# A long convolution with a gated projection on one core: PSUM tiles of one and two banks, one engine per first-stage group, GpSimd copying the real half

## The chip, the core and the metric

The kernel runs on one core of a Trainium2 chip. Five engines of the core work from queues of their own, each in order: TensorE (PE in the profile, with its weight loads as PEld) multiplies matrices, VectorE (DVE), ScalarE (ACT) and GpSimd (POOL) work elementwise, and SyncE (SP) issues the transfers between the large memory (HBM) and the on-chip memory SBUF. Matmuls write into a separate memory, PSUM, from which VectorE and ScalarE copy the results out; here it is cut into eight banks of 512 float32 values per partition. Engines wait for one another through semaphores, which the framework sets from the tiles that each instruction reads and writes.

The metric is the device time of one execution in microseconds, lower is better.

## The reference

Eight sequences of 6400 steps with 128 channels are convolved with a filter as long as they are, by a Fourier transform over twice the length; the result is gated and projected.

```python
def _attn_ref(x, h):                    # x (8, 6400, 128), h (6400, 128)
    L = 2 * S
    Xf = np.fft.rfft(x, n=L, axis=1)
    Hf = np.fft.rfft(h, n=L, axis=0)
    return np.fft.irfft(Xf * Hf[None], n=L, axis=1)[:, :S, :]

def _moe_ref(x, w_val, conv_w, w_out):  # x is the result above
    gate_pre[:, t] = sum over k of conv_w[k] * x[:, t - 4 + k]   # 5 taps, per channel
    gate = 1.0 / (1.0 + np.exp(-gate_pre))
    return (gate * (x @ w_val)) @ w_out
```

All arrays are float32.

## The kernel before

The length is split as 6400 = 100 x 64 (`N1`, `N2`), so that the transform becomes matmuls with small constant matrices, in four stages.

- **First stage** (`first_stage`, line 475): a transform of length 100 over one axis, in 16 groups of 8 channels per sequence. A group is 4 matmuls (8 instruction records in the trace, `ps<-r_sb,x`) into a *two-bank* PSUM tile; then four copies of 64 x 400 values bring it to `gy`, two by each of two steps `ev` (`j` = 0 and 1, one for each half of the partitions). Either step may go to ScalarE or VectorE.
- **Second stage** (`second`): a transform of length 64 for 13 groups `kb` of up to 8 frequencies, also into two banks (`ps<-gy,m`), followed by the product with the filter's spectrum. In `product` ScalarE copies the two halves, swapped, to a `w` tile, VectorE multiplies by the two spectrum tiles `h` (from HBM, 512 KB each), and GpSimd adds the two products into `gy`.
- **Third stage** (line 684 on): 32 groups of 4 channels, each 4 matmuls (8 records, `ps<-r_sb,gy`) into *one* bank, and one copy of 100 x 512 values to `dt` by ScalarE or VectorE.
- **Fourth stage**: 13 chunks of 5 (the first of 4) of the 64 columns (`ps<-m_sb,dt`), each into *one* bank; from that bank ScalarE and VectorE apply the five taps of the gate's convolution, with one addition by GpSimd. The function `gated` then applies the sigmoid, multiplies by the value projection (`ps<-y,w_sb`, *one* bank) and projects the product (`ps<-dt,w_sb` or `ps<-gl,w_sb`, *one* bank). Chunks from number 9 (`LAGGED`) on are copied out at once and finished later.

The **head** runs the first stage on the filter and on sequence 0, then 13 times `spectrum` (the filter's second stage, its real and imaginary halves written twice, once negated, to the `h` tiles and to HBM) with `direct` (sequence 0's second stage and product). In `spectrum` (line 611) ScalarE copies the real half from PSUM twice (`r0`, `r1_`) and the imaginary half negated (`i0`); GpSimd negates that in SBUF (`i1`). The first six groups of sequence 1 are stashed in the space of the table `m4`, and GpSimd copies them to `gy` later ("unstash").

After the head, for each sequence `b`: the third stage of `b` runs beside the first stage of `b + 1`, since the first stage overwrites parts of `gy` that the third stage has read, and then the fourth stage of `b` beside the second stage of `b + 1`. The third stage's copies to `dt` wait for all of the previous sequence's fourth stage and for its projections from `dt`.

**What sets the order.** Every step is added to a `_Plan` with a cost per engine it may run on, the steps it follows, a due time and its PSUM bank. `_Plan.forward` (line 196) simulates the engines with these costs: whenever an engine is free it takes the ready step that is due first and that fits. The order that comes out is written to the program, each instruction pinned behind those before it on its engine (`_InOrder`), so the chip keeps that order whatever its own times are. Due times come from the constants at the top: `PERIOD` per sequence, `THIRD`, `SECOND`, `FOURTH` for the spacing inside it, `GATE`, `LAGS`, `EARLY` for gating and chunks. The costs are `_act`, `_dve`, `_pool`, `_pe`, `_dma`.

**PSUM in the plan.** Four two-bank tiles (`places`, line 372) hold everything. `room` (line 309) gives a two-bank step the first pair of which both halves are free, and a one-bank step a half, a pair that is already half used first. A half is `places[i][:, h]`, a slice of the two-bank tile. `fits` keeps two engines from using a bank at the same time, except where their `side` masks differ, as those of the two first-stage `ev` steps do: the plan lets these run together.

Of the kernel before, what the change touches and what calls it, by code (L numbers as in the profile page):

```python
# [44 lines left out]
THIRD = 57000  # L45
FOURTH = 5150
SECOND = 4000
GATE = 15000
LAGS = 8200
EARLY = -1800  # L50
# [72 lines left out]
class _Op:  # L123
# [3 lines left out]
    def __init__(self, run, cost, after, bank=None, new=False, side=3, port=False):  # L127
        self.run, self.cost, self.bank, self.new, self.side, self.port = run, cost, bank, new, side, port
        self.after = [a for a in after if a is not None]
        self.rank = self.at = self.done = self.engine = None  # L130


class _Plan:
# [62 lines left out]
    def forward(self, places):  # L196
# [3 lines left out]
        halves = [[0] * 2 for _ in range(places)]  # L200
# [11 lines left out]
        def fits(o, e):  # L212
# [9 lines left out]
            return not any(x != e and s & o.side and t > now for x, s, t in b.seen)  # L222
# [5 lines left out]
        while left:  # L228
            moved = True
            while moved:  # L230
                moved = False
                for e in free:
# [27 lines left out]
                    if b is not None:  # L260
                        if o.new:
                            i, h = b.spot = self.room(b, halves, now)
                            for k in (0, 1) if b.n == 2 else (h,):
                                halves[i][k] = None
                        b.seen.append((e, o.side, now + dur))
# [10 lines left out]
                    heapq.heappush(events, (now + dur, -1, None))  # L276
                    moved = True
# [20 lines left out]
    def order(self, places):  # L298
        self.link()
        self.due()  # L300
        began, self.span = self.forward(len(places))
        for o in self.ops:
            if o.bank is not None:
                i, h = o.bank.spot
                o.bank.place = places[i] if o.bank.n == 2 else places[i][:, h]
        return began

    @staticmethod
    def room(b, halves, now):
        ok = [[t is not None and t <= now for t in p] for p in halves]  # L310
        if b.n == 2:
            return next(((i, 0) for i, p in enumerate(ok) if all(p)), None)
        one = [(i, p.index(True)) for i, p in enumerate(ok) if any(p)]
        return min(one, key=lambda x: (all(ok[x[0]]), x[0]), default=None)


def _act(n, ptr=False, held=False, sb=False):
    d = 150 + n / 1.2 + 95 * ptr + 45 * sb
# [26 lines left out]
def longconv_moe(ctx: ExitStack, tc: tile.TileContext, x, h, r1, m2, r3, m4, w64, out):  # L345
# [26 lines left out]
    places = [pp.tile([128, 2, 512], F32, name=f"ps_{i}") for i in range(4)]  # L372
# [102 lines left out]
    def first_stage(src, dst, before, base, step, groups=range(NG)):  # L475
        done = []
        for g in groups:
# [18 lines left out]
            for j in range(2):  # L496

                def ev(e, g=g, j=j, bank=bank):
                    v = bank.ap().rearrange("p b (m x) -> p b x m", x=SW)
# [459 lines left out]
```

## Time and profile before

| | us |
|---|---|
| median of 3 runs | 1389.91 (1385.95 to 1393.13) |
| the profiled execution | 1374.47 |
| its span, first to last instruction | 1372.7 |
| mean granted TensorE clock | 0.951 |
| one sequence, from one start of the fourth stage to the next (814.07 to 971.13) | 157.1 |

The profile comes from one execution; its time lies below the three runs of the table. The tables by stage give, for each stretch, the length, then for PE, PEld, DVE, ACT and POOL the busy time with the number of instructions, then the granted clock, the DMA share and the GB/s. A timeline row gives start, length, engine, line, operation, output and inputs, the number of merged instructions and, in brackets, how long the engine had been idle and what released it. Line 101 is the helper through which every instruction is issued, so groups are told apart by their tiles: `ps` is PSUM, buffer numbers are left out. PE is busy through most of the span; its busy time is that of pipelined matmuls, whose shown end includes some time that the next one overlaps.

### The profile page before, as it was taken

The page shows a single profiled execution, that of the slowest core. Times are in us where ns is not written, and L with a number is a line of the kernel's source. Part 1 is how long each engine was busy: PE and PEld are TensorE (multiplying, and loading weights), DVE is VectorE, ACT ScalarE, POOL GpSimd, SP SyncE. Part 2 cuts the span into 40 slices and gives each one's busy share as a digit, 9 for nine tenths or more (in the row PEclk, how much of TensorE's full clock was granted, in tenths as well). Part 3 has the DMA queues.
Part 4 walks back from the last instruction along what each step waited for, and adds up shares of the span by engine and source line. Part 5 has one row for each costly group of instructions (what it writes and reads, how often), then busy time and mean ns, then how long its engine had stood idle before and what let it go on. Part 6 is the DMA issues. An engine that isn't in the chain of part 4 may idle for free. (4 is left out here: it accounts for less than half of the span.)

```text
span 1372.7 us, 19881 instructions
## 1 busy us (share of the span) xinstructions
PE 1154.0 (84%) x7480; PEld 979.3 (71%) x7480; DVE 757.2 (55%) x1069; ACT 774.8 (56%) x1269; POOL 419.0 (31%) x239
## 2 busy tenths in 40 slices
PE   8986788788988889888887888888897888877785
PEld 8976787568875787668875787657875788755652
DVE  6874157643785358542775447652685437741254
ACT  5764467555764557455764557555673557633342
POOL 0396016410561016310462006510363105610011
PEclk9999999999999999699998999999997999989887
DMA  9578447722884248621684228732585217600011
GB/s 260 166 250 290 146 145 276 246 77 66 272 268 132 76 150 295 203 84 61 226 293 142 83 81 299 261 97 68 185 297 180 78 40 271 219 30 29 0 40 56
DMA packets 80460, 221.15 MB, mean 161 GB/s; under 512 B 9514, under 2 KB 24846, under 8 KB 80142
## 3 DMA queue, kind: packets, MB, share of 16 engines
q1 hardware_dynamic: 80366, 219.89, 49.3%
q8 instruction: 59, 0.97, 0.3%
q14 instruction: 35, 0.29, 0.1%
HBM read 184.47 MB, written 39.32 MB: 163 GB/s over the span
## 5 line engine op out<-in xcount | busy, mean ns | idle before, releaser
L101 PEld LDWEIGHTS ps<-r_sb,gy 128*100 128x100 f32 x2048 | 244.8, 173 | 100.9 <-ACT dt L101 37.9
L101 PEld LDWEIGHTS ps<-m_sb,dt 100*128 100x128 f32 x2048 | 258.7, 205 | 78.3 <-ACT w L101 16.8
L101 PE MATMUL ps<-r_sb,gy 128*100 128x128 f32 x2048 | 263.0, 278 | 51.4 <-ACT dt L101 22.5
L101 PE MATMUL ps<-m_sb,dt 100*128 100x100 f32 x2048 | 266.2, 290 | 42.1 <-ACT w L101 14.2
L101 DVE COPY gy<-ps 64x400 f32<-64x400 f32 x242 | 139.4, 576 | 287.9 <-ACT gy L101 284.2
L101 POOL TENSOR_TENSOR gy<-gy,w 128x1024 f32<-128x1024 f32 x96 | 239.0, 2495 | 143.8 <-DVE w L101 113.8
L101 ACT COPY dt<-ps 100x512 f32<-100x512 f32 (+2 forms) x286 | 160.7, 588 | 185.6 <-PE ps L101 164.0
L101 PE MATMUL ps<-r_sb,x 100*128 100x200 f32 x992 | 196.4, 344 | 46.6 <-issue 35.5
L101 PEld LDWEIGHTS ps<-gy,m 128*128 128x128 f32 x1600 | 195.2, 190 | 33.3 <-issue 16.0
L101 PEld LDWEIGHTS ps<-r_sb,x 100*128 100x128 f32 x992 | 169.7, 194 | 66.3 <-issue 55.9
L101 PE MATMUL ps<-gy,m 128*128 128x128 f32 x1600 | 204.1, 281 | 12.8 <-DVE gy L101 5.6
L101 DVE SCALAR_TENSOR_TENSOR dt<-ps,w_sb,dt 128x500 f32<-128x500 f32 (+7 forms) x216 | 133.3, 628 | 79.1 <-PE ps L101 51.1
L101 ACT COPY gy<-ps 64x400 f32<-64x400 f32 x246 | 119.3, 485 | 98.4 <-PE ps L101 93.8
L101 ACT COPY y<-ps 128x500 f32<-128x500 f32 x150 | 85.7, 576 | 120.0 <-PE ps L101 105.9
L101 ACT ACTIVATE w<-ps 64x1024 f32<-64x1024 f32 (+1 forms) x91 | 90.0, 989 | 84.1 <-DVE gy L101 47.8
L101 POOL TENSOR_TENSOR gl<-gl,q 128x500 f32<-128x500 f32 (+1 forms) x48 | 56.7, 1181 | 242.7 <-DVE gl L101 242.7
L101 DVE TENSOR_TENSOR gy<-ps,h 128x1024 f32<-128x1024 f32 (+1 forms) x100 | 116.3, 1173 | 18.9 <-PE ps L101 9.4
L101 DVE TENSOR_TENSOR w<-w,h 128x1024 f32<-128x1024 f32 (+1 forms) x91 | 126.4, 1399 | 0.0
L101 PE MATMUL ps<-y,w_sb 128*128 128x500 f32 x178 | 102.7, 661 | 17.5 <-DVE y L101 5.0
L101 POOL MEMSET dt<- 128x4 f32 x8 | 0.8, 105 | 378.0 <-PE ps L101 378.0
L101 POOL TENSOR_TENSOR dt<-dt,q 128x500 f32<-128x500 f32 (+1 forms) x64 | 84.5, 1320 | 101.2 <-DVE dt L101 101.0
L101 ACT COPY w<-ps 64x1024 f32<-64x1024 f32 (+2 forms) x95 | 90.7, 955 | 9.1 <-DVE dt L101 5.8
(53 smaller groups left out, 890.7 us busy)
## 6 DMA issues: line engine op xcount, KB each, us to landing
h<-hd SPq DMA_DIRECT2D x168, 512.0 KB, 4.8
m<-m SPq DMA_DIRECT2D x96, 512.0 KB, 5.2
x<-xl SPq DMA_DIRECT2D x116, 224.0 KB, 2.6
out<-y SPq DMA_DIRECT2D x89, 250.0 KB, 2.6
hd<-h SPq DMA_DIRECT2D x8, 512.0 KB, 3.5
hd<-hd SPq DMA_DIRECT2D x14, 256.0 KB, 3.8
h<-hd SPq DMA_DIRECT2D x14, 256.0 KB, 3.8
m_sb<-xl SPq DMA_DIRECT2D x12, 224.0 KB, 6.1
```

What stands on the lines that cost most here:

```text
L101: return self._tc.keep_in_program_order(call(*args, **kwargs))
```

## The change

- PSUM: two pair tiles stay. The other two pairs are tiles of a pool of their own in the head; at the first one-bank step this pool is closed and four one-bank tiles `pb_` take its place. `room` gives two-bank steps any pair before that moment and pairs 0 and 1 after it, and one-bank steps the four single tiles.
- First stage: one `ev` step makes all four copies of a group, on ScalarE or VectorE. The `side` masks are gone.
- `fits` counts a bank as in use until 45 ns (`HOP`) after an instruction on another engine ends.
- Head: GpSimd copies the real half in SBUF (after `r0`) in place of ScalarE's second PSUM copy, and ScalarE copies the imaginary half from PSUM in place of GpSimd's negation.
- Costs and constants: `_act`, the unstash cost, and six due-time constants. `PERIOD`, `HEAD_END` and all tile sizes in SBUF stay.

```diff
--- before.py
+++ after.py
@@ -42,12 +42,12 @@
 YB = 6
 HEAD_END = 101000
 PERIOD = 126600
-THIRD = 57000
-FOURTH = 5150
-SECOND = 4000
-GATE = 15000
-LAGS = 8200
-EARLY = -1800
+THIRD = 52500
+FOURTH = 5450
+SECOND = 4150
+GATE = 11750
+LAGS = 10260
+EARLY = -4600
 
 
 def _out_range(ch):
@@ -124,8 +124,8 @@
 
 
 
-    def __init__(self, run, cost, after, bank=None, new=False, side=3, port=False):
-        self.run, self.cost, self.bank, self.new, self.side, self.port = run, cost, bank, new, side, port
+    def __init__(self, run, cost, after, bank=None, new=False, port=False):
+        self.run, self.cost, self.bank, self.new, self.port = run, cost, bank, new, port
         self.after = [a for a in after if a is not None]
         self.rank = self.at = self.done = self.engine = None
 
@@ -193,11 +193,12 @@
                 if not need[id(u)]:
                     todo.append(u)
 
-    def forward(self, places):
+    def forward(self):
         need = {id(o): len(o.after) for o in self.ops}
         free = dict.fromkeys(("tensor", "scalar", "vector", "gpsimd", "sync"), 0)
         ready = {e: [] for e in free}
-        halves = [[0] * 2 for _ in range(places)]
+        halves = [[0] * 2 for _ in range(4)]
+        self.split = False
         port = server = now = 0
         events, began = [], []
         for o in self.ops:
@@ -219,7 +220,7 @@
                 return True
             if o.new:
                 return all(x.spot is not None for x in b.before) and self.room(b, halves, now) is not None
-            return not any(x != e and s & o.side and t > now for x, s, t in b.seen)
+            return not any(x != e and t > now for x, t in b.seen)
 
         for o in self.ops:
             if not need[id(o)]:
@@ -260,9 +261,10 @@
                     if b is not None:
                         if o.new:
                             i, h = b.spot = self.room(b, halves, now)
+                            self.split = self.split or b.n == 1
                             for k in (0, 1) if b.n == 2 else (h,):
                                 halves[i][k] = None
-                        b.seen.append((e, o.side, now + dur))
+                        b.seen.append((e, now + dur + self.HOP))
                         b.left -= 1
                         if not b.left:
                             i, h = b.spot
@@ -274,6 +276,7 @@
                     heapq.heappush(events, (o.done, self.index[id(o)], o))
                     heapq.heappush(events, (free[e], -1, None))
                     heapq.heappush(events, (now + dur, -1, None))
+                    heapq.heappush(events, (now + dur + self.HOP, -1, None))
                     moved = True
             if not left:
                 break
@@ -295,27 +298,25 @@
                 if not need[id(u)]:
                     wake(u)
 
-    def order(self, places):
+    def order(self):
         self.link()
         self.due()
-        began, self.span = self.forward(len(places))
-        for o in self.ops:
-            if o.bank is not None:
-                i, h = o.bank.spot
-                o.bank.place = places[i] if o.bank.n == 2 else places[i][:, h]
+        began, self.span = self.forward()
         return began
 
-    @staticmethod
-    def room(b, halves, now):
-        ok = [[t is not None and t <= now for t in p] for p in halves]
+    def room(self, b, halves, now):
+
+
+        free = [[t is not None and t <= now for t in p] for p in halves]
         if b.n == 2:
-            return next(((i, 0) for i, p in enumerate(ok) if all(p)), None)
-        one = [(i, p.index(True)) for i, p in enumerate(ok) if any(p)]
-        return min(one, key=lambda x: (all(ok[x[0]]), x[0]), default=None)
+            return next(((i, 0) for i, p in enumerate(free) if all(p) and (i < 2 or not self.split)), None)
+        if not self.split and not all(all(p) for p in free[2:]):
+            return None
+        return next(((i, h) for i in (2, 3) for h in (0, 1) if free[i][h]), None)
 
 
 def _act(n, ptr=False, held=False, sb=False):
-    d = 150 + n / 1.2 + 95 * ptr + 45 * sb
+    d = 155 + n / 1.2 + 112 * ptr + 35 * sb
     return d + 12 if held else d - 85, d
 
 
@@ -369,7 +370,10 @@
     x_sb = [cp.tile([PX, XG, N2], F32, name=f"x_{i}") for i in range(XB)]
     w_t = [cp.tile([128, KB * C], F32, name=f"w_{i}") for i in range(WB)]
     q_t = [cp.tile([128, CH, N1], F32, name=f"q_{i}") for i in range(2)]
-    places = [pp.tile([128, 2, 512], F32, name=f"ps_{i}") for i in range(4)]
+    early = tc.tile_pool(name="ep", bufs=1, space=bass.MemoryType.PSUM)
+    places = [[p.tile([128, 2, 512], F32, name=f"ps_{i}")] for p, i in ((pp, 0), (pp, 1))]
+    ep = early.__enter__()
+    places += [[ep.tile([128, 2, 512], F32, name=f"ps_{i}")] for i in (2, 3)]
     hd = dp.tile([NKB, 2, 2 * N2, KB * C], F32, name="hd")
     hx = h_sb + [dt[:, N1 * C + i * KB * C : N1 * C + (i + 1) * KB * C] for i in range(2)]
 
@@ -493,18 +497,18 @@
 
             p = add(mm, {"tensor": _pe(338, 4)}, [loads[n], r1_in], bank=bank, new=True)
             firsts.append(p)
-            for j in range(2):
-
-                def ev(e, g=g, j=j, bank=bank):
-                    v = bank.ap().rearrange("p b (m x) -> p b x m", x=SW)
+
+            def ev(e, g=g, bank=bank):
+                v = bank.ap().rearrange("p b (m x) -> p b x m", x=SW)
+                for j in range(2):
                     for c in range(2):
                         copiers[e](
                             dst(g)[c * N2 : (c + 1) * N2, 2 * j : 2 * j + 2],
                             v[j * N2 : (j + 1) * N2, :, c * N1 : (c + 1) * N1],
                         )
 
-                cost = {"scalar": _times(_act(400, held=True), 2), "vector": _times(_dve(400, held=True), 2)}
-                done.append(add(ev, cost, [p, *before(g)], bank=bank, side=1 << j))
+            cost = {"scalar": _times(_act(400, held=True), 4), "vector": _times(_dve(400, held=True), 4)}
+            done.append(add(ev, cost, [p, *before(g)], bank=bank))
         return done
 
 
@@ -617,12 +621,12 @@
         old = [hx_user[2 * kb + r - len(hx)] if kb >= 3 else [] for r in range(2)]
         cost = {"scalar": _act(n, held=True)}
         r0 = add(lambda e: nc.scalar.copy(t[0][:N2], v()[:N2]), cost, [p, *old[0]], bank=bank)
-        r1_ = add(lambda e: nc.scalar.copy(t[0][N2:], v()[:N2]), cost, [p, *old[0]], bank=bank)
+        r1_ = add(
+            lambda e: nc.gpsimd.tensor_copy(hs[0][N2:, :n], hs[0][:N2, :n]),
+            {"gpsimd": (170 + 0.86 * n,) * 2}, [r0, *old[0]],
+        )
         i0 = add(lambda e: nc.scalar.activation(t[1][:N2], v()[N2:], AF.Copy, scale=-1.0), cost, [p, *old[1]], bank=bank)
-        i1 = add(
-            lambda e: nc.gpsimd.tensor_scalar(out=hs[1][N2:, :n], in0=hs[1][:N2, :n], scalar1=-1.0, scalar2=None, op0=MUL),
-            {"gpsimd": (1250, 1250)}, [i0, *old[1]],
-        )
+        i1 = add(lambda e: nc.scalar.copy(t[1][N2:], v()[N2:]), cost, [p, *old[1]], bank=bank)
         full = kb < WHOLE
         st = [dma(hd[kb, 0, : 2 * N2 if full else N2, :n], hs[0][: 2 * N2 if full else N2, :n], n // (2 if full else 4), [r0, *([r1_] if full else [])])]
         if full:
@@ -717,7 +721,7 @@
                 plan.base = begin
                 ys1.append(add(
                     lambda e, g=g: nc.gpsimd.tensor_copy(gy_at(g), stash_at(g)),
-                    {"gpsimd": (1050, 1050)}, [*stashed[2 * g : 2 * g + 2], s3[2 * g], s3[2 * g + 1]],
+                    {"gpsimd": (860, 860)}, [stashed[g], s3[2 * g], s3[2 * g + 1]],
                 ))
             if b == 0:
                 m4_load(ys1, begin + 14000)
@@ -868,7 +872,7 @@
                 zero = []
                 for k, o in cells(0, n):
                     zero.append(add(
-                        lambda e, o=o: nc.gpsimd.memset(o[:, :, :1], 0.0), {"gpsimd": (110, 110)}, [p], bank=bank, side=0,
+                        lambda e, o=o: nc.gpsimd.memset(o[:, :, :1], 0.0), {"gpsimd": (110, 110)}, [p], bank=bank,
                     ))
                     parts.append((o[:, :, 1:], lambda k=k, pv=pv, m=o.shape[1]: pv()[:, k : k + m, : N1 - 1]))
                 first(4, parts, zero, 0, n)
@@ -909,8 +913,15 @@
         gated(0)
         dt_old = [*s4_new, *dt_new]
 
-    plan_ops = plan.order(places)
+    plan_ops = plan.order()
     for op in plan_ops:
+        if op.new:
+            i, k = op.bank.spot
+            if op.bank.n == 1 and len(places[2]) == 1:
+                early.__exit__(None, None, None)
+                sp = ctx.enter_context(tc.tile_pool(name="sp", bufs=1, space=bass.MemoryType.PSUM))
+                places[2:] = [[sp.tile([128, 512], F32, name=f"pb_{i}{h}") for h in range(2)] for i in (2, 3)]
+            op.bank.place = places[i][k]
         op.run(op.engine)
 
 
```

## The prediction

> **What bounds the kernel now.** I read the page first, then a table of busy time by stage, then the timeline inside each stage.
>
> ```profile
> PE 1154.0 (84%) x7480; PEld 979.3 (71%) x7480; DVE 757.2 (55%) x1069; ACT 774.8 (56%) x1269; POOL 419.0 (31%) x239
> ...
> DMA  9578447722884248621684228732585217600011
> GB/s 260 166 250 290 146 145 276 246 77 66 272 268 132 76 150 295 203 84 61 226 293 142 83 81 299 261 97 68 185 297 180 78 40 271 219 30 29 0 40 56
> ```
>
> The matrix engine (PE) is busy 1154.0 us of a span of 1372.7, so it idles 218.7 us. No other engine is near that, and the transfers are dense in part of each batch only. The average hides which wait ends last, so I cut the span into stages by the timeline's matmuls: the head's loop, phase A (third stage of a batch with the first stage of the next) and phase B (fourth stage with the next batch's second).
>
> ```profile
> core 0: us, PE busy (x) PEld busy (x) DVE busy (x) ACT busy (x) POOL busy (x), PEclk, DMA share, GB/s
> ...
> 51.00:123.80 72.80, 59.68 (x449) 57.64 (x449) 53.02 (x54) 48.65 (x61) 63.11 (x25) 0.95 0.77 245
> 123.80:184.00 60.20, 46.76 (x336) 42.52 (x337) 10.22 (x18) 26.82 (x51) 5.13 (x6) 1.00 0.54 173
> 814.00:897.00 83.00, 71.13 (x491) 59.25 (x489) 61.09 (x80) 54.02 (x78) 43.02 (x23) 0.96 0.76 254
> 897.00:971.00 74.00, 64.37 (x406) 55.22 (x407) 28.91 (x48) 38.29 (x74) 4.97 (x4) 0.98 0.26 76
> 1212.00:1278.00 66.00, 47.30 (x280) 34.99 (x280) 16.00 (x24) 24.90 (x45) 4.96 (x4) 0.96 0.07 27
> 1278.00:1372.70 94.70, 67.94 (x310) 46.84 (x310) 41.62 (x68) 33.97 (x62) 15.35 (x15) 0.79 0.09 35
> ```
>
> PE idles 13.1 us in the head's loop, 13.4 in the first phase A, 11.9 in a usual B (814 to 897), 9.6 in a usual A (897 to 971), 18.7 in the last A, 26.8 in the last B. In A both copying engines are half empty (ACT 38.3 of 74, DVE 28.9) and the DMA share is 0.26, so what stops PE there is not a full engine. The timeline shows what does. First, where nothing but the third stage runs:
>
> ```profile
> 126.49 1.12 PE L101 MATMUL ps<-r_sb,gy 128*100 128x128 f32 x8 [0.72 <-ACT dt L101]
> 127.65 0.59 ACT L101 COPY dt<-ps 100x512 f32<-100x512 f32 x1 [1.21 <-PE ps L101]
> 128.29 1.12 PE L101 MATMUL ps<-r_sb,gy 128*100 128x128 f32 x8 [0.68 <-ACT dt L101]
> 129.45 0.59 ACT L101 COPY dt<-ps 100x512 f32<-100x512 f32 x1 [1.21 <-PE ps L101]
> ...
> 148.07 1.12 PE L101 MATMUL ps<-r_sb,gy 128*100 128x128 f32 x8 [0.67 <-ACT dt L101]
> ...
> 811.84 1.04 PE L101 MATMUL ps<-r_sb,gy 128*100 128x128 f32 x8
> 812.71 1.52 PE L101 MATMUL ps<-r_sb,x 100*128 100x200 f32 x8
> 814.07 1.92 PE L101 MATMUL ps<-m_sb,dt 100*128 100x100 f32 x16
> ```
>
> Group, copy, group, copy, thirteen times at 1.80 us: each group waits for the copy of the one before, with all PSUM otherwise free. Yet `room` prefers a pair that is half used, so neighbouring groups lie in the two halves of one pair tile. The halves behave as one. Undisturbed, a third-stage group takes 0.87 us from start to start (811.84 to 812.71) and a first-stage group 1.36. The mixed part of A says the same:
>
> ```profile
> 303.83 1.91 PE L101 MATMUL ps<-r_sb,gy 128*100 128x128 f32 x16
> ...
> 304.03 0.98 ACT L101 COPY gy<-ps 64x400 f32<-64x400 f32 x2 [0.77 <-PE ps L101]
> 305.04 1.17 DVE L101 COPY gy<-ps 64x400 f32<-64x400 f32 x2 [3.65 <-ACT gy L101]
> 305.78 1.07 ACT L101 COPY dt<-ps 100x512 f32<-100x512 f32 x2 [0.77 <-PE ps L101]
> ...
> 306.31 1.59 PE L101 MATMUL ps<-r_sb,x 100*128 100x200 f32 x8 [0.57 <-issue]
> ...
> 310.23 1.59 PE L101 MATMUL ps<-r_sb,x 100*128 100x200 f32 x8 [0.57 <-issue]
> ```
>
> The copy of the first third-stage group starts at 305.78, when the second has ended too (303.83 + 1.91 = 305.74). The two engines that empty a first-stage group do so one after the other (ACT to 305.01, DVE from 305.04 to 306.21), although the planner lets them run side by side (`side`). PE's next first-stage group starts at 306.31, just after DVE ends: the planner thought that pair free over a microsecond earlier and gave it out again. The cycle takes 310.23 - 306.31 = 3.92 us and needs 1.36 + 2 x 0.87 = 3.10 of PE.
>
> **The change part by part.**
>
> *One-bank tiles.* Single banks become tiles of their own, so the chain of 1.80 us falls to PE's own 0.87 (ACT's copy, 0.59, hides beside the next group). First A: 13 x 0.93 = 12.1, and nine mixed cycles at 0.8 = 7, give 19, more than PE's idle 13.4, since a matmul's shown end includes 0.2 that the next overlaps; what is late next is the x loads and the m4 table. I take 14 (0 to 19). Usual A: PE idle 9.6, plus 0.2 at some 15 waits = 12.6. I take 10, six times, 60 (0 to 76). Last A: 32 groups x 0.87 + 11 gating matmul pairs of about 0.9 = 37.7 of 66; recoverable 28. The gating's own DVE and POOL steps come late next; I take 20 (0 to 28).
>
> *One engine empties a group.* ACT takes 4 x 0.49 = 1.96, DVE 4 x 0.58 = 2.33, in place of 0.98 + 1.17 in series (2.18 by the rows). The pair is held as long as before, and the planner now knows it. This is worth the 0.57 us wait above, counted in A already. The engine is now taken for about 2 us in a row, and third-stage copies queue behind it; four single banks give PE 4 x 0.87 = 3.5 us before it needs one of them, so that is hidden, and without that cover each of the 100 or so groups after the head would cost PE up to 1 us. I take 0 (from 0 to +100, the upper end being what rival (d) is about).
>
> *Head.*
>
> ```profile
> L101 POOL TENSOR_TENSOR gy<-gy,w 128x1024 f32<-128x1024 f32 x12 | 28.5, 2375 | 2.2 <-DVE w L101 1.4
> ...
> L101 POOL TENSOR_SCALAR h<-h 64x1024 f32<-64x1024 f32 x8 | 22.1, 2766 | 56.7 <-ACT h L101 56.2
> L101 DVE TENSOR_TENSOR w<-ps,h 64x1024 f32<-64x1024 f32 x16 | 19.6, 1222 | 10.0 <-POOL h L101 9.7
> L101 ACT COPY h<-ps 64x1024 f32<-64x1024 f32 x16 | 16.1, 1006 | 10.3 <-issue 4.6 <-PE ps L101 4.2 <-ACT dt L101 0.7
> ...
> L101 POOL COPY gy<-m_sb 128x800 f32<-128x800 f32 x6 | 5.1, 856 | 16.8 <-PE ps L101 14.0 <-issue 2.8
> ```
>
> Per step POOL does 2.77 + 2.38 = 5.15 us and the loop takes 72.8 / 13 = 5.6: POOL bounds it, and DVE waits for its negation. A GpSimd copy of 64x1024 does not occur; bounds are 0.86 (800 elements, 128 partitions) and 2.77 (the negation); I take 1.1, by the copy's 0.856 x 1024 / 800. POOL then needs 3.5 a step; ACT does three copies as before, one of them now for the imaginary half. The new waits: POOL's copy waits for ACT's first copy, and behind it on POOL's queue stand the adds of 2.38, for which the third stage and the reuse of the `w` tiles three steps on wait; DVE's product and SP's store wait for that copy as they waited for ACT's. POOL has 1.3 us of slack a step for it. Next late is PE (busy 59.7 of 72.8) and the DMA (72.8 x 245 GB/s = 17.8 MB; at the 300 GB/s of its densest slices 59 us). The loop goes to about 62: -11 (0 to -14).
>
> *Phase B.*
>
> ```profile
> 816.60 3.94 PE L101 MATMUL ps<-gy,m 128*128 128x128 f32 x32 [0.60 <-DVE gy L101]
> ...
> 841.29 2.03 PE L101 MATMUL ps<-gy,m 128*128 128x128 f32 x16
> ...
> 847.32 1.21 DVE L101 TENSOR_TENSOR gy<-ps,h 128x1024 f32<-128x1024 f32 x1
> ...
> 875.02 1.08 PE L101 MATMUL ps<-gy,m 128*128 128x128 f32 x8
> 878.47 3.47 PE L101 MATMUL ps<-m_sb,dt 100*128 100x100 f32 x20 [2.37 <-ACT w L101]
> 881.74 1.73 PE L101 MATMUL ps<-dt,w_sb 128*128 128x500 f32 x2
> 884.13 2.48 PE L101 MATMUL ps<-m_sb,dt 100*128 100x100 f32 x20 [0.67 <-ACT y L101]
> ...
> 888.86 2.48 PE L101 MATMUL ps<-m_sb,dt 100*128 100x100 f32 x20 [0.31 <-DVE gl L101]
> ...
> 894.13 1.87 PE L101 MATMUL ps<-y,w_sb 128*128 128x500 f32 x2
> ...
> 814.00:878.00 64.00, 56.86 (x422) 49.66 (x420) 50.44 (x65) 44.91 (x63) 35.67 (x18) 1.00 0.82 273
> 878.00:897.00 19.00, 14.27 (x69) 9.58 (x69) 10.66 (x16) 9.11 (x16) 7.34 (x5) 0.81 0.58 190
> ```
>
> Until 878 B moves 273 GB/s, near the page's best slices, so little goes there. The tail of 19 us holds three chunks (878.47, 884.13, 888.86) and four gating matmul pairs (881.74 to 894.13), about 3 x 2.3 + 4 x 0.9 = 10.5 of work, run at a granted clock of 0.81 with waits for banks (ACT y at 884.13): 8.5 lost, and 7.1 of idle before it. New chunk spacing and separate banks should spread it: I take 7 per B, 49 over seven (bounds: +25 each from the pairs, below, to -14). Last B, chains of DVE and POOL steps: 9 (0 to 20).
>
> The rest (new due-time constants, costs, the hop added to PSUM use) only orders the streams, SP's transfers among them, and is priced in B's bounds; the unstashing copies keep their 0.86 us; the new single/pair split waits once for two pairs to drain, when the head's copies end anyway. Sum: 11 + 14 + 60 + 20 + 49 + 9 = 163 us. The profiled execution took 1374.5 (span 1372.7 and 1.8 around it); it becomes 1211.5. The median shown is 15.4 above that execution; 1389.9 - 163 = 1227.
>
> **The rivals.** (a) *Everything comes.* A at its full 12.6, B's tail at its 10.5 of work with the clock up and 5.5 of the 7.1 before it, 14 each: 163 + 16 + 49 = 228, 1162. For it: one cause, the late release, repeats in all stages, and the clock falls only where PE idles. Against: B's 0.82 DMA share. After 2.37 us of idle at 876.1 the row at 878.47 takes 3.47 us for what takes about 2.4 at full clock. With the tail's 0.81 raised to 1 its 19 us would lose up to 3.6, 25 over seven, which (a) includes. [...]
>
> (b) *B does not move*, transfers and its chain of data holding it, and A gains less: 11 + 10 + 6 x 7 + 15 = 78, so 1312.
>
> (c) *The waits are not the tile's*, so that separate tiles do nothing and only the head and the pair given out too early (0.57 x about 10 cycles x 6 = 34) remain: 45, so 1345. Against it is the copy at 305.78, which waits for matmuls whose result it does not read. [...]
>
> (d) *Too few pairs: slower.* After the head, first- and second-stage groups have two pairs instead of up to four. A second-stage pair is held from 841.29 to 848.53, 7.2 us; two pairs then pass a group per 3.6, while the stage now passes one per (876.1 - 816.6) / 13 = 4.6. It decides from a hold of 9.2 us on. The other gains, 114 us, are eaten when B grows by 16.3, at a hold of 11.7; at 13 us B grows by 25, 175 in all, 1390 + 61 = 1451. Against it: ACT is busy 65% of B and DVE 74%, and the planner counts these pairs when it orders the queues.
>
> **How the numbers follow.** Forecast 1227 (own range 1180 to 1275) 0.55; (a) 0.18; (b) 0.15; (c) 0.06; (d) 0.06, of which 0.01 lands even. Low end 1150, a little under (a); high end 1320, past (b): 0.88 of the chance, less some 0.08 by which (a) and (b) scatter past the ends. A measurement of this kernel can tell about 0.5%. Faster by more 0.94, within 0.01, slower 0.05.
>
> **What would show it.** Right: third-stage groups 0.87 us apart instead of 1.80, a mixed cycle of about 3.1 to 3.2, phase A near 64 us, last A near 46, the head's loop near 62 with GpSimd copies near 1.1 us. Wrong: matmuls still waiting for the copy of another bank; B above 83 us with second-stage matmuls waiting for DVE's or ACT's release of a pair; GpSimd copies near 2.8.

## The result, and the profile after

The changed kernel takes 1082.09 us (median), the kernel before 1387.93 on the same chip: a ratio of 0.780, with a 95% interval of 0.776 to 0.785. The change saves 306 us where the prediction said 163. The direction was as forecast, and in phase A the mechanism too; the size was not, above all in phase B, and the time lies below the low end of the range.

These rows of the changed kernel's page are the busy totals, the granted clock, the DMA share and rate in 40 slices, and the shares of the chain that ended last:

```profile
PE 1050.1 (97%) x7480; PEld 938.2 (87%) x7480; DVE 765.9 (71%) x1028; ACT 787.5 (73%) x1310; POOL 389.5 (36%) x239
...
PEclk9999999999999999999999999999999999999999
DMA  8589958962499326982299634994269831891011
GB/s 247 153 294 298 316 155 305 326 215 90 129 322 344 133 86 224 329 291 94 70 317 330 208 91 131 322 338 139 86 221 318 294 106 35 302 319 49 27 49 74
...
PE 67%; DVE 8%; DMA 7%; ACT 3%; issue 3%; POOL 1%; SPq 0%; DVEq 0%; ACTq 0%; POOLq 0%
```

PE runs the same 7480 matmuls. Of a span of 1081.6 us it idles 31.5, where it idled 218.7: that is 187 us less. The other 104 us are missing from its *busy* time (1154.0 before, 1050.1 now). So a third of the gain came out of time in which PE was shown at work. The granted clock is 0.998 (0.951 before), and the best slices of the page (27 us long) move 344 GB/s where the best before (34 us long) moved 299.

The table by stage of the changed kernel, with the same columns as before: the head's loop, the first phase A, a usual B, the usual A behind it, the last A and the last B with the tail.

```profile
52.30:111.80 59.50, 55.83 (x451) 54.58 (x449) 56.09 (x59) 48.79 (x61) 41.74 (x25) 1.00 0.84 288
111.80:153.90 42.10, 42.10 (x337) 41.91 (x338) 11.76 (x17) 26.32 (x51) 5.13 (x6) 1.00 0.88 264
660.40:727.20 66.80, 64.90 (x488) 56.97 (x486) 57.70 (x72) 53.73 (x79) 40.79 (x23) 1.00 0.86 295
727.20:786.80 59.60, 59.60 (x409) 54.19 (x410) 32.27 (x48) 40.48 (x80) 5.93 (x5) 1.00 0.36 118
980.50:1019.30 38.80, 38.77 (x281) 32.87 (x281) 15.41 (x22) 24.59 (x44) 5.95 (x5) 1.00 0.11 41
1019.30:1081.60 62.30, 54.35 (x310) 38.26 (x310) 41.43 (x68) 34.52 (x62) 15.64 (x15) 0.96 0.15 56
```

In all three phases A PE has no idle time to speak of. A usual B has 1.9 us of it (11.9 before), and its transfers now run at 295 GB/s instead of 254, although the prediction held them to be near a ceiling.

Stage lengths of the two profiled runs, read from the starts of the stages' matmuls (the last B to the end of the last matmul), with the forecast beside them:

| stage | before | after | gain | forecast |
|---|---|---|---|---|
| head's loop | 72.8 | 59.5 | 13.3 | 11 |
| first A | 60.2 | 42.1 | 18.1 | 14 |
| six usual A, mean | 73.6 | 59.7 | 6 x 13.9 = 83 | 60 |
| last A | 65.8 | 38.8 | 27.0 | 20 |
| seven B, mean | 83.8 | 66.9 | 7 x 16.9 = 118 | 49 |
| last B | 89.6 | 58.6 | 31.0 | 9 |

The gains add up to 290.4, the difference of the two spans is 1372.7 - 1081.6 = 291.1. (The medians lie 306 apart; the profiled execution of the kernel before lay below its median, as the prediction noted.) Every stage gave more than forecast; of the 128 us missing from the forecast, 69 are in the usual B, 23 in the usual A, 22 in the last B and 14 in the rest.

The timeline of the changed kernel: the start of the first phase A, then one and a half mixed cycles of a usual A.

```profile
111.79 13.81 PE L101 MATMUL pb<-r_sb,gy 128*100 128x128 f32 x120 [2.12 <-ACT m_sb L101]
...
648.83 1.91 PE L101 MATMUL pb<-r_sb,gy 128*100 128x128 f32 x16
649.03 1.98 ACT L101 COPY gy<-ps 64x400 f32<-64x400 f32 x4 [1.12 <-PE ps L101]
649.90 0.69 DVE L101 COPY dt<-pb 100x512 f32<-100x512 f32 x1 [1.54 <-PE pb L101]
650.58 1.52 PE L101 MATMUL ps<-r_sb,x 100*128 100x200 f32 x8
650.78 0.69 DVE L101 COPY dt<-pb 100x512 f32<-100x512 f32 x1 [0.18 <-PE pb L101]
651.93 1.91 PE L101 MATMUL pb<-r_sb,gy 128*100 128x128 f32 x16
```

Fifteen third-stage groups (120 records) run without a gap in 13.81 us, 0.9 each where the chain before took 1.80. In the mixed part the cycle is 651.93 - 648.83 = 3.10 us, as forecast. One copy of a third-stage group starts at 649.90 while the next group still runs, and ACT empties the whole first-stage group in 1.98 us beside them; both used to wait for a neighbour.

### The profile page after: what moved, and what is told of

Read it like the earlier page. It is cut to its first block, busy times and chain, and to the rows that moved or that the text cites. A ratio compares the mean times of both kernels' runs of the same rounds, so it can differ in the third digit from the quotient of the medians.

```text
span 1081.6 us, 19637 instructions
## 1 busy us (share of the span) xinstructions
PE 1050.1 (97%) x7480; PEld 938.2 (87%) x7480; DVE 765.9 (71%) x1028; ACT 787.5 (73%) x1310; POOL 389.5 (36%) x239
## 4 chain that ended last, share of the span: by engine, by line
PE 67%; DVE 8%; DMA 7%; ACT 3%; issue 3%; POOL 1%; SPq 0%; DVEq 0%; ACTq 0%; POOLq 0%
PE pb L101 46%; PE ps L101 22%; DMA h<-hd 4%; DVE gy L101 3%; DMA m<-m 2%; DVE dt L101 2%; DVE w L101 2%; ACT w L101 2%; DVE gl L101 1%; DMA out<-y 1%; ACT y L101 1%; ACT dt L101 1%; POOL gl L101 0%; DVE y L101 0%; POOL gy L101 0%
## 5 line engine op out<-in xcount | busy, mean ns | idle before, releaser
L101 ACT COPY gy<-ps 64x400 f32<-64x400 f32 x456 | 222.0, 487 | 106.1 <-PE ps L101 102.1
L101 PEld LDWEIGHTS pb<-r_sb,gy 128*100 128x100 f32 x2048 | 242.1, 171 | 48.7 <-issue 45.7
L101 PEld LDWEIGHTS pb<-m_sb,dt 100*128 100x128 f32 x2048 | 239.1, 192 | 22.1 <-issue 15.8
L101 PE MATMUL pb<-r_sb,gy 128*100 128x128 f32 x2048 | 249.8, 273 | 7.7 <-DVE gy L101 4.6
L101 PE MATMUL pb<-m_sb,dt 100*128 100x100 f32 x2048 | 241.1, 274 | 0.3 <-DVE dt L101 0.2
L101 PEld LDWEIGHTS ps<-gy,m 128*128 128x128 f32 x1600 | 194.0, 188 | 35.1 <-DVE gy L101 16.9
L101 DVE COPY dt<-pb 100x512 f32<-100x512 f32 x164 | 113.3, 691 | 144.1 <-PE pb L101 126.0
L101 DVE SCALAR_TENSOR_TENSOR dt<-pb,w_sb,dt 128x500 f32<-128x500 f32 (+7 forms) x216 | 132.1, 627 | 12.4 <-issue 4.8
L101 ACT COPY y<-pb 128x500 f32<-128x500 f32 x141 | 80.1, 571 | 49.4 <-PE pb L101 45.2
L101 PE MATMUL pb<-y,w_sb 128*128 128x500 f32 x178 | 91.2, 594 | 2.4 <-DVE y L101 1.5
L101 ACT COPY w<-ps 64x1024 f32<-64x1024 f32 (+1 forms) x91 | 88.4, 972 | 1.7
```

The source lines that it names most:

```text
L101: return self._tc.keep_in_program_order(call(*args, **kwargs))
```

## The experiments

The theory is that two halves of one two-bank tile wait for each other as one tile, that the planner's order does not know this, and that this sets the idle time in A and in B alike. The rivals are that the order, the due times or the single engine brought the gain, and, for B, that its transfers hold it. Stage lengths of an experiment are read as in the table above. Each ratio is to the kernel before on the same chip, where its median was 1377.50 to 1380.93 us (1387.93 with the result above), so a difference to the changed kernel's 1082 can be off by some 10 us.

### The same order on halves of pair tiles

The changed kernel with its plan, its order and its banks as they are; only the four single banks are halves of two pair tiles again.

```diff
-                places[2:] = [[sp.tile([128, 512], F32, name=f"pb_{i}{h}") for h in range(2)] for i in (2, 3)]
+                both = [sp.tile([128, 2, 512], F32, name=f"pb_{i}") for i in (2, 3)]
+                places[2:] = [[t[:, h] for h in range(2)] for t in both]
```

> The order on every queue is that of the changed kernel; only the four one-bank tiles are slices of two two-bank tiles again. Theory L (a pair tile's halves wait for each other, and that alone cost most of the 306 us): third-stage groups in a chain of 1.80 us again, 1280 to 1400 us. Theory P (the planner's better picture of the chip, its order and its due times, gave most): at most 1150 us.

Measured: 1360.56 us, a ratio of 0.985 [0.976, 0.995] to the kernel before. The same instructions in the same order lose 278 of the 306 us. The table by stage of this run, for the first A, a usual A and the usual B behind it:

```profile
111.40:167.40 56.00, 46.84 (x336) 41.57 (x337) 11.00 (x17) 26.17 (x51) 5.11 (x6) 1.00 0.63 200
...
722.80:795.60 72.80, 66.08 (x408) 55.77 (x409) 30.95 (x48) 40.60 (x80) 5.96 (x5) 0.95 0.29 92
795.60:880.00 84.40, 72.34 (x488) 62.71 (x487) 57.15 (x72) 54.23 (x78) 43.60 (x23) 0.90 0.70 238
```

B takes 84.40 where the changed kernel takes 66.80, for 488 matmuls in both. PE's idle time makes 10.2 of these 17.6 us (84.40 - 72.34 = 12.1 against 1.9), its busy time the other 7.4. The clock is enough for the second part: 64.90 us of work at a granted clock of 0.90 would be 72.1, and the row has 72.34. The timeline of this run shows both parts, at the start of the first A and in a B:

```profile
114.15 1.12 PE L101 MATMUL pb<-r_sb,gy 128*100 128x128 f32 x8 [0.80 <-ACT dt L101]
115.31 0.58 ACT L101 COPY dt<-pb 100x512 f32<-100x512 f32 x1 [1.21 <-PE pb L101]
115.95 1.12 PE L101 MATMUL pb<-r_sb,gy 128*100 128x128 f32 x8 [0.68 <-ACT dt L101]
117.11 0.58 ACT L101 COPY dt<-pb 100x512 f32<-100x512 f32 x1 [1.21 <-PE pb L101]
...
642.68 3.89 PE L101 MATMUL ps<-gy,m 128*128 128x128 f32 x32
...
650.77 4.56 PE L101 MATMUL pb<-m_sb,dt 100*128 100x100 f32 x20 [4.20 <-DVE dt L101]
...
657.42 3.79 PE L101 MATMUL ps<-gy,m 128*128 128x128 f32 x16 [2.09 <-DVE gy L101]
```

The chain of 1.80 us is back to the hundredth. In B a chunk waits 4.20 us for VectorE's taps, and then its 20 matmuls take 4.56 us. The same place of the changed kernel's timeline:

```profile
664.37 3.89 PE L101 MATMUL ps<-gy,m 128*128 128x128 f32 x32
668.09 2.37 PE L101 MATMUL pb<-m_sb,dt 100*128 100x100 f32 x20
670.30 2.04 PE L101 MATMUL ps<-gy,m 128*128 128x128 f32 x16
```

With the same order and the same banks there is no wait, and the 20 matmuls take 2.37 us.

### The layout alone

The kernel before with the new `places`, `room` and split; its costs, due times, head and two `ev` steps stay.

```diff
+        free = [[t is not None and t <= now for t in p] for p in halves]
         if b.n == 2:
-            return next(((i, 0) for i, p in enumerate(ok) if all(p)), None)
...
+            return next(((i, 0) for i, p in enumerate(free) if all(p) and (i < 2 or not self.split)), None)
...
+        return next(((i, h) for i in (2, 3) for h in (0, 1) if free[i][h]), None)
...
-    places = [pp.tile([128, 2, 512], F32, name=f"ps_{i}") for i in range(4)]
+    early = tc.tile_pool(name="ep", bufs=1, space=bass.MemoryType.PSUM)
+    places = [[p.tile([128, 2, 512], F32, name=f"ps_{i}")] for p, i in ((pp, 0), (pp, 1))]
```

> The kernel before with the layout alone: two pair tiles and four one-bank tiles after the head, everything else as before, due times too. Theory L: most of the gain, 1090 to 1170 us. Theory P: 1270 us or more.

Measured: 1166.33 us, 0.848 [0.844, 0.852]: 211 us from this part alone. A falls from 73.6 to 68.0, the last A from 65.8 to 38.9, B from 83.8 to 69.0 and the last B from 89.6 to 57.3. B thus gets 14.8 of its 16.9 us with the old due times and from the layout by itself.

### Everything but the layout

The changed kernel with four pair tiles and the old `room`, ordered anew by the planner for them.

```diff
-        return next(((i, h) for i in (2, 3) for h in (0, 1) if free[i][h]), None)
+        one = [(i, p.index(True)) for i, p in enumerate(ok) if any(p)]
+        return min(one, key=lambda x: (all(ok[x[0]]), x[0]), default=None)
...
-            op.bank.place = places[i][k]
+            op.bank.place = places[i] if op.bank.n == 2 else places[i][:, k]
```

> The changed kernel planned and laid out with the four two-bank tiles of before, whose halves serve one-bank steps; all else as changed. Theory L: 1300 to 1390 us. Theory P: at most 1150 us.

Measured: 1314.74 us, 0.958 [0.950, 0.966]. All other parts together are worth 63 us without the layout. B is 81.9, A 71.0.

### Half the transfers in B

The kernel before, with the second half of each `h` tile left out of the loads after the head, so that the product uses stale values there. If the transfers hold B, B must shrink.

```diff
-            h_in.append(dma(h_sb[n % HB][:, :k], hd[kb, r, :, :k], k // 2, [*after, *stored[kb][r]], 6000))
+            h_in.append(dma(h_sb[n % HB][:, : k // 2], hd[kb, r, :, : k // 2], k // 2, [*after, *stored[kb][r]], 6000))
```

> The kernel before, in which each load of the filter's spectrum after the head fetches only the first half of each tile (the product then uses stale values in the other half); the order on the queues is the same. The forecast gave phase B little because it moves 273 GB/s. If transfers hold B: B falls from 83.8 to 75 us or less, 1320 us or less. If the waits between the halves of a pair hold it (theory L): B stays within 2 us, 1365 to 1390 us.

Measured: 1383.55 us, 1.002 [0.998, 1.006]. The row of the table by stage for the stretch that the prediction took as its usual B:

```profile
814.00:897.00 83.00, 72.53 (x471) 61.16 (x472) 59.16 (x76) 52.03 (x74) 42.98 (x23) 0.89 0.53 169
```

The DMA share is 0.53 instead of 0.76, the rate 169 GB/s instead of 254, and B's mean length stays: 84.3 (83.8 before). In the kernel before, the transfers did not hold it.

### Two steps again

The changed kernel with two `ev` steps per first-stage group and the `side` masks, so that the planner again believes two engines empty a pair side by side.

```diff
-            def ev(e, g=g, bank=bank):
-                v = bank.ap().rearrange("p b (m x) -> p b x m", x=SW)
-                for j in range(2):
+            for j in range(2):
+
+                def ev(e, g=g, j=j, bank=bank):
+                    v = bank.ap().rearrange("p b (m x) -> p b x m", x=SW)
...
-            done.append(add(ev, cost, [p, *before(g)], bank=bank))
+                done.append(add(ev, cost, [p, *before(g)], bank=bank, side=1 << j))
```

> The changed kernel with a first-stage group emptied in two steps that the planner takes to run side by side, as before. Theory L: the mixed cycle of phase A goes from 3.1 us back towards 3.9 where the pair is handed out too early, 9 cycles in 7 phases, 1110 to 1140 us. Theory P in the form that the planner's knowledge of this emptying gave most: 1200 us or more. If the pair's early release costs nothing now: 1082.

Measured: 1158.77 us, 0.839 [0.833, 0.845]; 77 us slower than the changed kernel, more than expected. A takes 67.2 (59.7), B 70.3 (66.9), the first A 50.1 (42.1). The timeline in a usual A:

```profile
691.38 0.98 ACT L101 COPY gy<-ps 64x400 f32<-64x400 f32 x2 [1.58 <-PE ps L101]
...
692.39 1.17 DVE L101 COPY gy<-ps 64x400 f32<-64x400 f32 x2 [2.74 <-ACT gy L101]
693.66 1.59 PE L101 MATMUL ps<-r_sb,x 100*128 100x200 f32 x8 [0.57 <-issue]
...
696.30 1.17 DVE L101 COPY gy<-ps 64x400 f32<-64x400 f32 x2 [2.75 <-ACT gy L101]
697.57 1.59 PE L101 MATMUL ps<-r_sb,x 100*128 100x200 f32 x8 [0.57 <-issue]
```

VectorE's half waits for ScalarE's half again, PE gets the pair 0.57 us late, and the cycle is 697.57 - 693.66 = 3.91 us, the 3.92 of the kernel before, although every third-stage group has a tile of its own. So the layout takes away the waits of third-stage groups, and the single engine those for the first-stage pair. Two steps that the planner knows to run one after the other were not tried, so how much is the plan's wrong belief and how much the handover between two engines stays open; the two halves in series take 2.18 us here (691.38 to 693.56) and the single engine 1.98, which leaves little to the handover.

### One engine alone

The kernel before with one `ev` step and its unstash following that one step.

```diff
-                cost = {"scalar": _times(_act(400, held=True), 2), "vector": _times(_dve(400, held=True), 2)}
-                done.append(add(ev, cost, [p, *before(g)], bank=bank, side=1 << j))
+            cost = {"scalar": _times(_act(400, held=True), 4), "vector": _times(_dve(400, held=True), 4)}
+            done.append(add(ev, cost, [p, *before(g)], bank=bank))
```

> The kernel before with the first-stage group emptied by one engine alone. The pair handed out too early costs 0.57 us in some 10 cycles of 6 phases and is known to the planner now: 1340 to 1370 us. If this emptying is where the gain came from: 1200 us or less. If the halves' waits hide it: 1388.

Measured: 1332.69 us, 0.969 [0.962, 0.976]: 45 us better. The usual A falls from 73.6 to 65.3 and the last B from 89.6 to 84.9, while the first A grows from 60.2 to 70.0; B (83.9) and the last A (65.9), which has no first stage beside it, do not move.

### The due times: old in the changed kernel, new in the kernel before

```diff
-THIRD = 52500
+THIRD = 57000
...
-EARLY = -4600
+EARLY = -1800
```

> The changed kernel with the six due-time constants of before. Theory L: 1082 to 1120 us, a matter of order alone. Theory P in the form that the retuned constants matter most: 1200 us or more.

Measured for the changed kernel with all six old constants: 1122.72 us, 0.814 [0.808, 0.820], 41 us slower than with the new ones and a little past the 1120 expected. Most of it is in B: 72.0 against 66.9, seven times 5.1. The reverse edit, the six new constants in the kernel before:

> The kernel before with the six due-time constants of the changed one and nothing else. In the changed kernel they were worth 41 us, nearly all in phase B. If they act through the order alone: 1340 to 1355 us. If they fit only the new layout: 1370 to 1400 us.

Measured: 1409.53 us, 1.021 [1.014, 1.027]. The new constants make the kernel before *slower*, by 29 us (A 76.6, B 86.6), past the range of both expectations. What they are worth depends on the other parts of the change, and no run shows on which. The layout need not be it: everything but the layout, new constants included, gains 63 us, more than one engine alone (45) and the new head alone (7) together. The stage lengths point at the single engine. On pair tiles, B with the new constants is 86.6 where two engines empty a group and 81.9 where one does (83.8 and 83.9 with the old ones); with the new layout and the old constants, B is 69.0 with two engines and 72.0 with one. These runs differ in the head and the costs too, so this is not shown.

### The head: old in the changed kernel, new in the kernel before

```diff
-            lambda e: nc.gpsimd.tensor_copy(hs[0][N2:, :n], hs[0][:N2, :n]),
...
+        r1_ = add(lambda e: nc.scalar.copy(t[0][N2:], v()[:N2]), cost, [p, *old[0]], bank=bank)
...
+        i1 = add(
+            lambda e: nc.gpsimd.tensor_scalar(out=hs[1][N2:, :n], in0=hs[1][:N2, :n], scalar1=-1.0, scalar2=None, op0=MUL),
...
-        i1 = add(lambda e: nc.scalar.copy(t[1][N2:], v()[N2:]), cost, [p, *old[1]], bank=bank)
```

> The changed kernel with the head's copies as before (ScalarE copies the real half twice, GpSimd negates the imaginary half). If GpSimd's 5.15 us a step bounds the loop: 11 to 14 us more, 1093 to 1096 us. If transfers or the matrix engine bound it all the same: 1082 to 1085 us.

Measured: 1095.64 us, 0.794 [0.787, 0.800]; 13.5 us slower than the changed kernel, and the loop takes 72.0 instead of 59.5. The new head in the kernel before:

> The kernel before with the head's copies alone changed. GpSimd bounds the head's loop: 1374 to 1378 us. If it does not: 1386 to 1390 us.

Measured: 1370.92 us, 0.995 [0.992, 0.998]. The loop falls to 58.8, 14 us less, but only 6.6 (3 to 11 by the interval) reach the end. In its profile the first A and the usual A stand as they were within 1 us, while B takes 85.2 instead of 83.8, about 10 us over seven, and the last B 91.7 instead of 89.6. Why is not shown; the seven B of the kernel before already lie between 81.4 and 87.1. The copies behind it, in the costliest groups of the changed kernel:

```profile
L101 POOL COPY h<-h 64x1024 f32<-64x1024 f32 x8 | 8.3, 1034 | 57.5 <-ACT h L101 57.1
```

A copy takes 1034 ns where the negation took 2766.

### One pair, three pairs

Rival (d) said that two pairs are too few. Here the changed kernel has one pair and six singles, then three pairs and two singles; the edit is the bound in `room`, and `places` to match.

```diff
-            return next(((i, 0) for i, p in enumerate(free) if all(p) and (i < 2 or not self.split)), None)
+            return next(((i, 0) for i, p in enumerate(free) if all(p) and (i < 1 or not self.split)), None)
...
-        return next(((i, h) for i in (2, 3) for h in (0, 1) if free[i][h]), None)
+        return next(((i, h) for i in (1, 2, 3) for h in (0, 1) if free[i][h]), None)
```

> The changed kernel with one pair tile and six one-bank tiles after the head, planned so. Rival (d) of the forecast by its own arithmetic: a second-stage group holds the pair 7.2 us, so 13 groups need 94 us and B grows by about 27; a first-stage group holds it about 4 us, so phase A grows to 64 or more: about 1280 to 1320 us. If pairs are not scarce: 1082 to 1100 us.

Measured: 1310.52 us, 0.949 [0.943, 0.955]. B takes 108.6 us, 42 more; A falls to 50.2 because first-stage groups of the next sequence slip into B. The time lies in the range expected, but by luck: B was to grow by 27 and A to grow too. The timeline at the end of a B, where the second stage runs almost alone:

```profile
685.40 2.82 PE L101 MATMUL ps<-gy,m 128*128 128x128 f32 x16 [2.55 <-DVE gy L101]
...
692.43 3.01 PE L101 MATMUL ps<-gy,m 128*128 128x128 f32 x16 [2.55 <-DVE gy L101]
698.83 3.78 PE L101 MATMUL ps<-gy,m 128*128 128x128 f32 x16 [3.38 <-DVE gy L101]
706.05 3.78 PE L101 MATMUL ps<-gy,m 128*128 128x128 f32 x16 [3.45 <-DVE gy L101]
...
718.74 2.12 PE L101 MATMUL ps<-gy,m 128*128 128x128 f32 x16 [3.40 <-DVE gy L101]
```

From the first of these rows to the fourth, three groups take 706.05 - 685.40 = 20.65 us: one pair passes a group per 6.9. So the prediction's hold of 7.2 us is about right, and two pairs can pass a group per 3.4 to 3.6, while B in the changed kernel asks for one per 66.8 / 13 = 5.1.

> The changed kernel with three pair tiles and two one-bank tiles after the head, planned so. A chunk holds its bank some 7 us and gating needs two more in turn, so with two single banks phase B grows by 20 us or more: 1200 us or more. If single banks are not scarce and pairs are: below 1082 us.

Measured with three pairs and two singles: 1241.22 us, 0.899 [0.893, 0.904]. A is even a little shorter (56.3), but B takes 88.4 and the last B 90.2. The timeline of a B shows PE waiting for a single bank that ScalarE still reads:

```profile
623.21 3.09 PE L101 MATMUL pb<-m_sb,dt 100*128 100x100 f32 x20 [1.96 <-ACT y L101]
...
659.62 4.71 PE L101 MATMUL pb<-m_sb,dt 100*128 100x100 f32 x40 [0.67 <-ACT y L101]
```

None of these versions is faster than the changed kernel.

## Why the prediction was right in direction and too small

**What bounds the kernel: right.** The reading of the rows at 126.49 to 129.45, that the halves of a pair wait for each other as one tile, is shown by the same order on halves: the chain of 1.80 us comes and goes with the identity of the tile, at the same banks. The run on halves goes through the banks in the same order as the changed kernel, and in the chain there no copy runs beside the next group's matmuls: at 115.95 PE has waited 0.68 us for ScalarE, where the changed kernel runs fifteen groups without a gap in 13.81 us. Here the tile decides, not the bank. The reading of the rows at 305.04 and 306.31, the pair given out too early, is borne out by the two steps, which bring the cycle of 3.91 us back. Rival (c) falls with the first.

**One-bank tiles in A: right, with the sizes set too low.** First A: the chain of rows gave 19 and I cut it to 14 because PE idled only 13.4; it gave 18.1. Usual A: 10 with an upper end of 12.6, and it gave 13.9. Last A: 20 of a recoverable 28, and it gave 27. In the first and the usual A the step that failed is to take PE's idle time as nearly all that can be had: "PE idle 9.6, plus 0.2 at some 15 waits". The same matmuls are busy 64.37 us in the A before and 59.60 after, so 4.8 of busy time went with the waits, not 3. The clock of 0.98 there accounts for about 1.2 (59.60 / 0.98 = 60.8), and overlap of the shown ends (1.04 us at 811.84 for a group that takes 0.87) probably for the rest: in the first A the busy time falls by 4.7, from 46.76 to 42.10, at a granted clock of 1.00 in both. In the last A the 28 were counted from PE's work, and the 8 held back for the gating's own VectorE and GpSimd steps were not needed.

**One engine: right about the 0.57 us wait, wrong to think that the layout brings that gain too.** I took 0 for this part because the wait was "counted in A already". But of A's gain the layout alone brings 5.6 (73.6 to 68.0); with two steps in the changed kernel A stays at 67.2, and the kernel takes 77 us more. The queueing behind the 2 us step, priced at up to +100, did not show: PE has no idle time in A.

**The head: right.** -11 within 0 to -14; the loop gave -13.3. The copy was taken as 1.1 us and took 1.03.

**Phase B: the step that failed.** "Until 878 B moves 273 GB/s, near the page's best slices, so little goes there." I took 7 per B with a bound of 14, and 9 for the last; they gave 16.9 and 31. Two things were wrong. The rate was read as a ceiling, but it was the pace that PE's waits allowed: with half of the `h` loads B keeps its length, and once the waits are gone the whole B moves 295 GB/s. And I looked for the shared tiles mainly in the tail after 878. The view of PE's waits in the same B of the kernel before (engine and tile, what it waited for, us in total, times, the longest) shows what held it:

```profile
PE ps L101 <- DVE dt L101: 3.8, 6, 1.5
PE ps L101 <- ACT w L101: 2.4, 1, 2.4
PE ps L101 <- DVE gy L101: 1.9, 2, 1.3
PE ps L101 <- DVE gl L101: 1.2, 2, 0.9
PE ps L101 <- ACT q L101: 0.9, 1, 0.9
PE ps L101 <- DVE y L101: 0.8, 1, 0.8
PE ps L101 <- ACT y L101: 0.7, 1, 0.7
```

They add up to 11.7 us, nearly all of the 11.9 us of idle time in that B, and no transfer is among them: all are waits for VectorE or ScalarE, and the most time goes to the taps and gating steps that use single banks (`dt`, `gl`, `q`, `y`: 7.4). The layout alone returns 14.8 of the 16.9 us. Here, too, more came back than the idle time: from 83.00 to 66.80 us the idle time falls by 10.0 and the busy time by 6.2. The last B, taken as a chain of VectorE and GpSimd steps, is the same case: 57.3 with the layout alone. In its rows with the tail, idle time falls from 26.8 to 7.9 us and busy time from 67.9 to 54.4, at a granted clock of 0.79 before and 0.96 after; the prediction counted neither the slow clock nor the waits for a shared tile there.

**Due times: no price of their own, and not small.** The prediction let them go as what "only orders the streams" and put them into B's bounds. The constants alone are worth 41 us in the changed kernel and minus 29 in the kernel before, so the term depends on the other parts; on which, no run shows.

**The sum.** The parts do not add. Alone, the layout brings 211, one engine 45, the head 7 and the due times -29 us, 234 in all; together 306 (about 297 against the medians of the kernel before in these experiments). The layout itself has three prices: 211 us added alone, 233 taken from the changed kernel under a new plan, 278 taken from it under the same plan. That each wait that is left hides part of what the other parts free is the likely reading, not a measured one.

**The rivals.** (a), "everything comes", was nearest at 1162 and still 80 us too high, since it kept the same bound on A and on B. (b) falls with B, which did move; the half loads show that its transfers had not held it. (d) holds for one pair and not for two: one pair passes a group per 6.9 us, so two pass one per 3.4, and B asks for one per 5.1.

**What stays open.** Of B's loss on halves, 10.2 us are idle and 7.4 are busy time, as much as the slower clock would take. Slow matmuls stand behind idle stretches there (20 in 4.56 us behind 4.20 us, 16 in 3.79 behind 2.09), so the second part most likely follows from the first, but no run took the idle time away and kept the clock down. Which sharing in B costs most, that of chunk with chunk or of chunk with gating, was not tried either. Nor were the new costs and the 45 ns added to PSUM use tried by themselves.

## What to carry to other kernels

Give each thing that is used by itself a tile of its own: in this kernel a slice of a larger PSUM tile is waited for as the whole tile, whatever banks lie under it (a third-stage group per 1.80 us on halves, per 0.9 on tiles of their own). An order worked out by a planner is only as good as its picture of what is serialised, and constants tuned beside one set of changes can cost time without them (29 us here), so tune them again after each. Neither the idle time of the busiest engine nor a transfer rate seen under waits was a bound here on what removing the waits brought: the busy time held a slowed clock and probably overlapped ends (PE's fell from 1154.0 to 1050.1 us, while the clock rose from 0.951 to 0.998), and the rate was what the waiting engine asked for (254 GB/s in a B before, 295 after).

## What the hardware showed beyond that

In these runs slow matmuls and a low granted clock stand behind PE's waits, but the length of the last wait alone does not decide it. On the halves, 4.20 us of idle time are followed by 20 matmuls in 4.56 us instead of 2.37; the granted clock of the whole B that holds them (638.7 to 722.8) is 0.90. With one pair, idle stretches of 2.55 us stand ahead of 16 matmuls in 2.82 and 3.01 us, and stretches of 3.38 and 3.45 us ahead of 16 in 3.78 us, which take 2.04 undisturbed; yet behind 3.40 us, at 718.74, they take 2.12. The mean granted clock of these two runs is 0.923 and 0.907. In the kernel before, 20 chunk matmuls take 3.47 us at 878.47 and 2.51 us at 559.97, both behind 2.37 us of idle time, and 4.59 us at 564.86 behind 0.66 us. From 565 to 575 the granted clock is 0.50 although PE is busy for 9.16 of the 10 us, so the prediction's "the clock falls only where PE idles" is too narrow. What else decides it is not shown.

The transfer rate was unexpected too: 295 GB/s over the 66.8 us of a B and up to 344 in a slice of the page, where no slice of the kernel before, each about a quarter longer, went over 299.
